# Fused attention, mixture of experts and gated MLP: a store that the first gathers no longer wait for, w_out loaded behind it, fillers moved

## The chip, the cores and the metric

The kernel runs on one core of a Trainium2 chip. The metric is the device time of one execution in microseconds (us). Before the change three runs took 814.79, 814.86 and 816.84 us; their median is 814.86 us.

## The reference

Three parts run one after the other: sparse attention (scores more than `tau` below the row's maximum are dropped), a mixture of eight experts in which a token may keep its predecessor's expert, and a gated MLP whose `w_sg` mixes the 576 tokens of a batch.

```python
scores = np.where(scores >= thresh, scores, -1e9)       # thresh: the row's maximum - tau
x = softmax(scores) @ v                                 # [4, 8, 576, 64] -> x [4, 576, 512]
...
e = fresh_e if s == 0 or local_gate[b, s] < 0.5 else prev_e
out[b, s] = p[e] * (np.maximum(x[b, s] @ w1[e], 0.0) @ w2[e])
...
h = gelu(x @ w_in); u, v = h[..., :512], h[..., 512:]
v_n = (v - mu) / np.sqrt(var + 1e-06) * g_ln
v_s = np.einsum('ts,bsd->btd', w_sg, v_n) + b_sg[None, :, None]
out = x + (u * v_s) @ w_out
```

## The kernel before

**Three stages.** Attention runs over pairs of heads and halves of the four batches (`Attn`); batches 0 and 1 are done first, 2 and 3 second. `Route` then sorts the 2304 tokens by expert into 22 tiles of 128 rows (`CAPS` gives the experts 5, 3, 3, 3, 2, 2, 2 and 2 tiles, in the order of a rank that is computed on the chip). `Tail.moe` gathers each tile's tokens from `x_dram` by an indirect DMA, multiplies by the expert's `w1` and `w2` as sums of three rounded products (a "high" and a "low" part of each operand), and stores each tile of results to the DRAM tensor `ys`. `Tail.mlp` gathers token tiles from `ys`, scales them by the gate's probability, transposes them and runs the gated MLP; it goes over two passes `p`: p = 0 is batches 0 and 1, p = 1 is batches 2 and 3, nine tiles of 128 tokens each.

**What sets the order.** All operations go into one graph (`Graph`, `Flow`) with an engine, a planned duration and a due time. `order` places them by a list schedule, and every engine then executes its own list strictly in that order. The waits between engines are put in afterwards by the framework, from what each instruction reads and writes, in the order in which the planner emits them. A gather from `ys` reads the whole tensor by this reckoning, since its rows are known only on the chip.

**The places that the change touches.**

- `Attn.keep`, two fillers on TensorE at the end of attention: six small products each of the identity with itself, whose result nobody reads.
- `Route.half` and `Route.rest`: small VectorE operations that count tokens by expert, rank the experts (`key`, `rank`), and turn the rank into tile numbers.
- `plain`, the first expert's first two tiles, unsplit: eight products "A1" (128x256) and eight "A2" (128x512), which fill TensorE while routing runs on VectorE. A1 reads the cell `c_78`, and a later chunk of `w2` is loaded into that cell.
- `second` and `put`: the second product of an expert and the store of its tile (`yst`). `self.yst` is the list of the 22 stores.
- `s_weights`: loads of the MLP's weights, among them two loads of `w_out` (from `wo32`, the copy in fp32) and their split into parts.
- `group`: for three token tiles each, the gather, the scaling `xpg` (VectorE), the transposes `xT` (TensorE), the split `xh` (ScalarE) and `xl` (VectorE), then per tile the product `vp` (twelve 128x512 matmuls) and a gelu (`sq`, `sqh`, `tanh`, `gelu`). The gather waits for all the stores:

```python
g.gather(W(need - self.P['mgth']), gth, r=[self.iu], w=[xu], deps=self.yst + [g.more], name="gth")
```

- `a.side`: during attention, zeros are stored to the spare tiles of `ys`, behind tile 22.

Most lines of the trace say L183, a helper through which `Tail`'s instructions go; there an instruction is told by its operands. `MF`, `MR`, `c` and `r` are parts of SBUF, `PS` is PSUM.

## Time and profile before

| | us | |
|---|---|---|
| median of three runs | 814.86 | 814.79 to 816.84 |
| the profiled execution | 814.26 | 0.60 under the median |
| its span, first to last instruction | 812.5 | 1.76 lies around it |
| TensorE (PE) busy | 771.8 | 95% of the span |
| VectorE (DVE) busy | 608.2 | 75% |
| ScalarE (ACT) busy | 461.5 | 57% |
| GpSimd (POOL) busy | 257.0 | 32% |
| mean granted clock of TensorE | 0.987 | 1 is 2.4 GHz, 0.5 is 1.2 GHz |

Times in the trace count from the first instruction. The page cuts the span into 40 slices and gives the busy share of each engine in tenths. TensorE stands at 9 nearly everywhere; the lowest slice, a 4, lies where the experts end and the MLP begins (some 569 to 589 us), and the granted clock is below 9 there alone.

### The profile page before, as it was taken

How to read it: one execution, taken by the hardware profiler on the slowest of the kernel's cores; microseconds unless marked ns; L12 is line 12 of the kernel's file. 1: busy time of each engine (PE TensorE's matmuls, PEld its weight loads, DVE VectorE, ACT ScalarE, POOL GpSimd, SP SyncE). 2: the span in 40 equal slices, each digit the busy share in tenths (PEclk: the TensorE clock that was granted, in tenths of full speed). 3: DMA queues.
4: the chain of work that ended last, by engine and by line, in shares of the span. 5: the costliest groups of instructions: out<-in, count | busy, mean ns of one | idle time of the engine just before them, and what ended most of it. 6: DMA issues, size and time to landing. Idle time of an engine off the chain costs nothing.

```text
span 812.5 us, 13654 instructions
## 1 busy us (share of the span) xinstructions
PE 771.8 (95%) x4813; PEld 658.3 (81%) x4814; DVE 608.2 (75%) x1293; ACT 461.5 (57%) x941; POOL 257.0 (32%) x348
## 2 busy tenths in 40 slices
PE   7899999999979999999999999999499999999997
PEld 4687877878667877598998988999388999899996
DVE  7999999999989985767668688774289753587732
ACT  5788988889848983354434455554336631256410
POOL 5232333332222300413524432224682143121410
PEclk9999999999999999999999999999799999999999
DMA  7232414453253012878576587644620012200011
GB/s 226 87 121 63 136 59 150 153 172 102 79 184 96 30 40 104 295 226 289 173 248 212 182 250 256 218 153 165 186 65 1 1 52 79 91 14 1 15 40 65
DMA packets 46909, 103.17 MB, mean 127 GB/s; under 512 B 7536, under 2 KB 7536, under 8 KB 46832
## 3 DMA queue, kind: packets, MB, share of 16 engines
q1 hardware_dynamic: 43632, 91.72, 34.3%
q0 software_dynamic: 3200, 10.49, 4.1%
q8 instruction: 40, 0.66, 0.3%
q14 instruction: 37, 0.30, 0.1%
HBM read 80.17 MB, written 22.02 MB: 126 GB/s over the span
## 4 chain that ended last, share of the span: by engine, by line
PE 52%; DVE 2%; issue 1%; DMA 1%; ACT 1%; POOL 0%; DVEq 0%
PE PS L183 52%; DVE MF L183 1%; DVE r L183 1%; DMA MF<-ys,MF 0%; ACT r L183 0%; ACT MF L183 0%; DVE c L183 0%; DMA ys<-MF 0%; DVE bs L183 0%; POOL MF L183 0%; DVE mv L183 0%; DVE rq L183 0%; DVE rqi L183 0%; DVEq L183 0%
## 5 line engine op out<-in xcount | busy, mean ns | idle before, releaser
L183 PE MATMUL PS<-r,r 128*128 128x512 f32 (+2 forms) x1512 | 298.3, 355 | 0.7 <-DVE MF L183 0.3
L183 PEld LDWEIGHTS PS<-r,r 128*128 128x128 f32 x1512 | 258.2, 190 | 32.4 <-DVE r L183 2.2
L425 PE MATMUL PS<-MR 128*128 128x288 f32 x640 | 114.3, 316 | 9.9 <-DVE MF L459 7.0
L459 DVE SCALAR_TENSOR_TENSOR MF<-PS,MF 128x576 f32<-128x576 f32 x144 | 116.8, 812 | 8.5 <-ACT MF L450 5.9
L450 ACT ACTIVATE MF<-PS,MF 128x576 f32<-128x576 f32 x144 | 107.5, 747 | 6.8 <-DVE MF L436 4.7
L430 DVE TENSOR_REDUCE MF<-PS 128x1 f32<-128x576 f32 x144 | 104.6, 752 | 8.8 <-PE PS L425 7.5
L425 PEld LDWEIGHTS PS<-MR 128*128 128x128 f32 x640 | 91.2, 191 | 18.8 <-DVE MF L459 11.3
L183 PE MATMUL PS<-MR,r 128*128 128x256 f32 (+2 forms) x616 | 101.6, 322 | 0.0
L183 PEld LDWEIGHTS PS<-MR,r 128*128 128x128 f32 x616 | 91.6, 188 | 8.1
L183 ACT ACTIVATE r<-PS 128x512 fp32r<-128x512 f32 (+2 forms) x102 | 49.1, 499 | 85.2 <-PE PS L183 82.1
L372 ACT ACTIVATE c<-PS 128x512 f32<-128x512 f32 (+1 forms) x160 | 82.5, 565 | 14.2 <-PE PS L479 13.9
L479 PE MATMUL PS<-ident,MF 128*128 128x128 f32 x576 | 81.7, 277 | 7.4 <-ACT c L372 7.0
L183 ACT ACTIVATE MF<-PS 128x512 f32<-128x512 f32 (+1 forms) x64 | 35.7, 558 | 77.1 <-PE PS L183 63.0
L479 PEld LDWEIGHTS PS<-ident,MF 128*128 128x128 f32 x576 | 65.8, 141 | 13.4 <-ACT c L372 11.0
L183 DVE TENSOR_TENSOR r<-c,r 128x1024 fp32r<-128x1024 f32 x42 | 56.2, 1368 | 16.4 <-ACT r L183 16.3
L183 DVE SCALAR_TENSOR_TENSOR r<-PS,r 128x384 fp32r<-128x384 f32 (+1 forms) x64 | 31.3, 489 | 45.3 <-ACT r L183 41.5
L183 DVE SCALAR_TENSOR_TENSOR MF<-MF,PS 128x384 f32<-128x384 f32 (+1 forms) x84 | 50.1, 606 | 16.2 <-ACT MF L183 15.7
L183 ACT ACTIVATE r<-c 128x1024 fp32r<-128x1024 f32 x46 | 46.8, 1055 | 15.1 <-PE PS L183 6.6
L183 POOL TENSOR_SCALAR MF<-MF 128x512 f32<-128x512 int32 x12 | 20.3, 1695 | 106.8 <-DVE MF L183 47.4
L404 POOL TENSOR_TENSOR MR<-c,MR 128x576 fp32r<-128x576 f32 x29 | 41.3, 1424 | 39.3 <-ACT MR L372 22.6
L183 ACT ACTIVATE r<-MF 128x256 fp32r<-128x256 f32 (+1 forms) x48 | 15.7, 359 | 62.2 <-DVE MF L183 62.2
L445 POOL TENSOR_TENSOR MF<-MF,cB 128x1 f32<-128x1 f32 x64 | 13.0, 204 | 117.4 <-DVE MF L430 108.1
(226 smaller groups left out, 1110.1 us busy)
## 6 DMA issues: line engine op xcount, KB each, us to landing
c<-in_w_dram SPq DMA_DIRECT2D x64, 512.0 KB, 4.8
c<-in_kP_dram SPq DMA_DIRECT2D x32, 288.0 KB, 3.1
c<-in_qP_dram SPq DMA_DIRECT2D x32, 288.0 KB, 3.1
ys<-MF SPq DMA_DIRECT2D x36, 256.0 KB, 3.5
x_dram<-c SPq DMA_DIRECT2D x6, 768.0 KB, 3.6
MF<-in_w_in_dram SPq DMA_DIRECT2D x8, 512.0 KB, 5.4
c<-in_vP_dram SPq DMA_DIRECT2D x12, 320.0 KB, 4.1
out_dram<-MF SPq DMA_DIRECT2D x12, 256.0 KB, 2.0
```

The source lines that it names most:

```text
L183: return lambda *a, **k: x(*[v(y) for y in a], **{n: v(y) for n, y in k.items()})
L372: self.nc.scalar.activation(out, src, AF.Copy, **k)
L404: e.tensor_tensor(l, self.raw(u)[1], h.bitcast(F32), op=ALU.subtract)
L425: self.nc.tensor.matmul(self.PS[:, banks[hf], 0:288], q, k[:, 288 * hf:288 * hf + 288], start=(n == 0), stop=(n == len(ops) - 1))
L430: self.nc.vector.tensor_reduce(m, self.tl[i]["s"], axis=AX.XY, op=ALU.max)
L445: self.nc.gpsimd.tensor_tensor(self.nbt(i)[:, 1:2], self.tl[i]["m"], self.cB[:, 1:2], op=ALU.add)
L450: self.nc.scalar.activation(e.rearrange("p (a b) -> p a b", a=2), t["s"], AF.Exp, bias=self.nbt(i)[:, 0:1], scale=0.125)
L459: self.nc.vector.scalar_tensor_tensor(w.rearrange("p (a b) -> p a b", a=2), t["s"], self.nbt(i)[:, 1:2], t["e"].rearrange("p (a b) -> p a ...
L479: self.nc.tensor.transpose(p[:, c, :], t["w"][:, z + c * 128:z + (c + 1) * 128], self.cst["ident"])
```

## The change

- The rank of the experts is broken at equal tile counts by the number of tokens of the first two batches instead of by the expert's number, so that the last expert in rank has few of them; if it has more than 128 of them its capacity falls by one tile (`f2`, `last`). So the last tile of the 22 holds tokens of batches 2 and 3 only. This is three small VectorE operations more.
- The gathers of pass p = 0 wait for all stores but the last one. Those of p = 1 wait for all, as before.
- The two loads of `w_out` also wait for the last store.
- `keep` is gone. In its place stand five fillers `idle` of the same six products, behind the last expert's last product.
- Zeros are stored to tile 21 as well (15 stores of zeros in place of 14; the first two go together).

```diff
-    KEEP = 6.949
...
-    def keep(self, banks):
-        x = self.cst["ident"].bitcast(BF16)
-        for _ in range(6):
-            self.nc.tensor.matmul(self.PS[:, banks[0], 0:256], x[:, 0:128], x[:, 0:256])
...
-        k = add("keep", "PE", 0.645, 18 * NPH / 2 * per + self.KEEP, lambda bk: self.keep(k.banks), [("av", NPH // 2 - 1, 1, 1)], 1)
-        k.users.append(add("keep2", "PE", 0.645, 18 * NPH / 2 * per + self.KEEP, lambda: self.keep(k.banks), [("rec", NPH // 2 - 1, 2)]))
...
-            k.append(op("DVE", 8, lambda: v.scalar_tensor_tensor(self.k0, fs, 1024.0, cst["cE"], op0=ALU.mult, op1=ALU.add), o))
+            k.append(op("DVE", 8, lambda: v.scalar_tensor_tensor(self.k0, fs, 1048576.0, ka, op0=ALU.mult, op1=ALU.add), o))
+            k.append(op("DVE", 8, lambda: v.tensor_scalar(self.f2, ca, 128.5, None, op0=ALU.is_gt), o))
...
-        o = op(8, lambda: v.scalar_tensor_tensor(key[:, :, 0], rt, 8.0, self.k0, op0=ALU.mult, op1=ALU.add), o)
+        o = op(8, lambda: v.scalar_tensor_tensor(key[:, :, 0], rt, 16384.0, self.k0, op0=ALU.mult, op1=ALU.add), o)
...
+        o3 = op(8, lambda: v.scalar_tensor_tensor(last, rank, 6.5, self.f2, op0=ALU.is_gt, op1=ALU.mult), o)
+        o1 = op(8, lambda: v.tensor_tensor(cap, cap, last, op=ALU.subtract), o1, o3)
...
+        p, o = Bank(), last
+
+        def idle():
+            x = ident.bitcast(BF16)
+            for _ in range(6):
+                nc.tensor.matmul(p.ap[:, 0:256], x[:, 0:128], x[:, 0:256])
+
+        for _ in range(5):
+            o = g.op("PE", 0.645, W(T + 6), idle, deps=[o], pw=p, name="idle")
+        p.first.users.append(o)
...
-            g.op("DQ", 1.46, V(P["wo"] - 6), ..., w=[wr], deps=self.conv, name="sld")
+            g.op("DQ", 1.46, V(P["wo"] - 6), ..., w=[wr], deps=self.conv + self.yst[-1:], name="sld")
...
-                g.gather(W(need - self.P['mgth']), gth, r=[self.iu], w=[xu], deps=self.yst + [g.more], name="gth")
+                g.gather(W(need - self.P['mgth']), gth, r=[self.iu], w=[xu], deps=(self.yst if p else self.yst[:-1]) + [g.more], name="gth")
...
+        zero = lambda *t: [nc.sync.dma_start(out=ys[k * 128:(k + 1) * 128, :], in_=z) for k in t]
+        a.side = [lambda: zero(NT - 1, NT)] + [lambda k=k: zero(k) for k in range(NT + 1, NT + NOV)]
```

**SP's list at the end of the experts.** SP issues the loads and stores. `ys<-MF` is a tile's store, `c_77<-wo` and `c_79<-wo` are the loads of `w_out`; `DMASW` semaphores count the indirect DMAs of GpSimd (0 and 1 are here the first two gathers of the MLP), `DMAHW` those of SP, eight in turn. Before:

```order
L183 DMA c_75<-in_w_sgT_dram 64x576
L183 DMA ys<-MF 128x512 [waits Activation_49]
L183 DMA c_77<-wo_60 128x2x512 [waits Pool_49]
L183 DMA ys<-MF 128x512 [waits Activation_49]
L183 DMA c_79<-wo_60 128x2x512 [waits DMAHW4_49,Pool_49]
```

and with the change:

```order
L183 DMA c_75<-in_w_sgT_dram 64x576
L183 DMA ys<-MF 128x512 [waits Activation_49]
L183 DMA ys<-MF 128x512 [waits DMASW1_49,DMASW0_49,Activation_49]
L183 DMA c_77<-wo_60 128x2x512 [waits Pool_49]
L183 DMA c_79<-wo_60 128x2x512 [waits DMAHW5_49,Pool_49]
```

Both loads of `w_out` moved behind the last store, and the last store waits for two gathers.

**GpSimd's list at the same place.** `MF<-ys` are gathers, `MR<-c` is the split of a part of `w_sg`. Before:

```order
L183 TENSOR_TENSOR MR<-c_79,MR 128x576 [waits DMAHW4_49,DMAHW7_49,PE_49,Activation_49]
L183 TENSOR_TENSOR MR<-c_78,MR 128x576 [waits DMAHW5_49,PE_49,Activation_49]
L183 DMA MF<-ys,MF 128x512 [waits DMAHW6_49,DMAHW3_49,DMAHW1_49]
L183 DMA MF<-ys,MF 128x512 x2
L183 DMA MF<-ys,MF 128x512 [waits DMASW3_49]
```

and with the change:

```order
L183 TENSOR_TENSOR MR<-c_79,MR 128x576 [waits DMAHW0_49,DMAHW5_49,PE_49,Activation_49]
L183 DMA MF<-ys,MF 128x512 [waits DMAHW7_49,DMAHW6_49,DMAHW2_49]
L183 DMA MF<-ys,MF 128x512
L183 DMA MF<-ys,MF 128x512 [waits DMAHW3_49]
L183 DMA MF<-ys,MF 128x512 [waits DMASW3_49]
```

The split of `c_78` moved behind the seventh gather. Counted in turn, the last store is the user of `DMAHW3` in both programs: before, the first gather names it; now the third does, and the first names `DMAHW2`, the store before the last.

**TensorE's and VectorE's lists at the end of attention.** On TensorE the routing's transposes and products (L1056, L1059, L1066, L1067 before) stand between the fillers (L305) and the products A1. Before:

```order
L1056 MATMUL PS<-ident,MF 9x9
L305 MATMUL PS<-ident 128x256
...
L1059 MATMUL PS<-ident,MF 128x9
L305 MATMUL PS<-ident 128x256
...
L1066 MATMUL PS<-MF 128x80
L1067 MATMUL PS<-MF 128x80
L183 MATMUL PS<-c_78,c_74 128x256
```

and with the change (each `c_78,c_74` begins one A1 of four matmuls):

```order
L1049 MATMUL PS<-ident,MF 9x9
L183 MATMUL PS<-c_78,c_74 128x256
...
L1052 MATMUL PS<-ident,MF 128x9
L183 MATMUL PS<-c_78,c_74 128x256
...
L1059 MATMUL PS<-MF 128x80
L1060 MATMUL PS<-MF 128x80
L183 MATMUL PS<-c_79,c_71 128x512 x4
L183 MATMUL PS<-c_78,c_71 128x512 x4
```

In VectorE's list one weight split moved into the routing, between the scan and the operation that follows it:

```order
L1050 TENSOR_REDUCE MF<-PS 9x1
L1051 SCALAR_TENSOR_TENSOR MF<-MF 9x128
L183 TENSOR_TENSOR r_3214<-c_79,r_3214 128x1024
L1053 TENSOR_SCALAR MF<-PS 128x9
L1054 TENSOR_TENSOR MF<-MF 128x8x9
```

Two A1 took the fillers' places, the A2 moved up ahead of the routing's turns, and the split that stood behind the routing stands in it.

## Rows read from the trace of the kernel before

**Rows 1.** Stages: us, busy us of PE, PEld, DVE, ACT, POOL, clock, DMA share, GB/s.

```profile
347.78:575.13 227.35, 227.09 (x1292) 205.62 (x1292) 156.87 (x222) 107.08 (x161) 81.00 (x59) 1.00 0.65 216
575.13:585.99 10.86, 0.00 (x0) 0.03 (x1) 0.48 (x1) 5.79 (x8) 5.28 (x6) 0.70 0.66 203
593.23:610.74 17.51, 16.93 (x94) 15.00 (x92) 15.76 (x29) 8.65 (x17) 15.58 (x20) 1.00 0.08 27
```

**Rows 2.** The chain of waits that ended last: start us, us, what.

```profile
610.74 18.25 PE PS L183 x94
```

**Rows 3.** Timeline of SP's queue at the last stores.

```profile
574.42 0.58 SPq L183 DMA_DIRECT2D ys<-MF  x1
575.04 0.43 SPq L183 DMA_DIRECT2D c<-wo  x1
575.77 0.32 SPq L183 DMA_DIRECT2D ys<-MF  x1
```

**Rows 4.** DMA, us to landing: stores at 550.3, 574.4, 575.7; gather at 583.3.

```profile
ys<-MF SPq DMA_DIRECT2D x1, 256.0 KB, 2.0
...
ys<-MF SPq DMA_DIRECT2D x1, 256.0 KB, 2.8
...
ys<-MF SPq DMA_DIRECT2D x1, 256.0 KB, 5.5
...
MF<-ys,MF POOLq DMA_INDIRECT x1, 3.5
```

**Rows 5.** Timeline of POOL: gathers 1, 3 and 6, then the splits.

```profile
581.99 1.03 POOL L183 DMA_INDIRECT MF<-ys,MF  x1 [4.19 <-issue]
...
584.58 0.95 POOL L183 DMA_INDIRECT MF<-ys,MF  x1 [0.30 <-issue]
...
588.50 0.95 POOL L183 DMA_INDIRECT MF<-ys,MF  x1 [0.31 <-issue]
...
593.23 7.41 POOL L183 TENSOR_TENSOR MR<-c,MR 128x576 fp32r<-128x576 f32 x5
600.72 4.94 POOL L183 TENSOR_TENSOR r<-c,r 128x1024 fp32r<-128x1024 f32 x2
```

**Rows 6.** Timeline of DVE: sixth scaling, first gelu step, eighth scaling.

```profile
592.32 0.48 DVE L183 TENSOR_SCALAR MF<-MF 128x512 f32<-128x512 f32 x1 [0.71 <-DMA MF<-ys,MF]
594.29 0.69 DVE L183 SCALAR_TENSOR_TENSOR MF<-MF,PS 128x512 f32<-128x512 f32 x1 [1.49 <-ACT MF L183]
...
601.27 2.13 DVE L183 TENSOR_SCALAR c<-c,MF 128x512 f32<-128x512 f32 x1
```

**Rows 7.** Timeline of PE: first vp, then second and third vp with the first up.

```profile
588.49 5.13 PE L183 MATMUL PS<-r,r 128*128 128x512 f32 x12
...
593.82 9.92 PE L183 MATMUL PS<-r,r 128*128 128x512 f32 x48
```

**Rows 8.** As rows 1, where the granted clock rises again.

```profile
593.00:593.20 0.20, 0.20 (x2) 0.18 (x1) 0.00 (x0) 0.00 (x0) 0.20 (x1) 0.84 0.90 123
```

**Rows 9.** Timelines of PE, DVE and ACT at the end of attention.

```profile
316.38 1.89 PE L183 MATMUL PS<-c,c 128*128 128x256 f32 x8
...
318.30 0.83 PE L305 MATMUL PS<-ident 128*128 128x256 bf16 x6
...
327.70 1.29 PE L1204 MATMUL PS<-MF 128*128 128x20 bf16 x36 [0.31 <-DVE MF L1197]
...
342.14 4.74 PE L183 MATMUL PS<-r,MR 128*128 128x384 f32 x24
...
319.39 0.17 DVE L1060 TENSOR_SCALAR MF<-PS 128x9 int32<-128x9 int32 x1 [0.32 <-PE PS L1059]
...
332.79 1.22 DVE L183 TENSOR_TENSOR r<-c,r 128x1024 fp32r<-128x1024 f32 x1
...
339.03 1.89 DVE L183 TENSOR_TENSOR r<-PS,r 128x512 fp32r<-128x512 f32 x3
...
318.59 1.05 ACT L183 ACTIVATE r<-c 128x1024 fp32r<-128x1024 f32 x1
```

More of the change, by code (lines that the diff above doesn't have):

```diff
@@ L998, in __init__ @@
         self.pg = self.sp[:, 1, :]
-        self.es, self.first, self.least, self.k0, self.c2, self.d2, self.rc = m([128, 1]), m([128, 8]), m([128, 8]), m([128, 8]), m([128, 8]), m([128, 8]), m([128, 8], I32)
+        self.es, self.first, self.least, self.f2, self.k0, self.c2, self.d2, self.rc = m([128, 1]), m([128, 8]), m([128, 8]), m([128, 8]), m([128, 8]), m([128, 8]), m([128, 8]), m([128, 8], I32)
         self.pe = h2(lambda: m([128, 9, 8]))
@@ L1161, in rest @@
         ovx, cE, rc = cst["ovx"], cst["cE"], self.rc
-        rt, key, cmp_, rank, cap, base, ov, oc, dl, pk = t([128, 8], I32), t([128, 8, 1]), t([128, 8, 8]), t([128, 8]), t([128, 8]), t([128, 8]), t([128, 8]), t([128, 9]), t([128, 8]), t([128, 1, 8, 1])
+        rt, key, cmp_, rank, last, cap, base, ov, oc, dl, pk = t([128, 8], I32), t([128, 8, 1]), t([128, 8, 8]), t([128, 8]), t([128, 8]), t([128, 8]), t([128, 8]), t([128, 8]), t([128, 9]), t([128, 8]), t([128, 1, 8, 1])
         osel, pt, bT, cT, dT, os_, tl = t([128, 2, 8, 9]), t([128, 18], I32), t([128, 18], I32), t([128, 18], I32), t([128, 18], I32), t([128, 18]), t([128, 18, 1], BF16)
@@ L1397, in mm @@
                             nc.tensor.matmul(p.ap, x[:, f, :], y[:, s], start=(f == 0 and n == 0), stop=(f == 7 and n == 2))
-                g.op("PE", pe(512, 6), W(T), mm, r=[hu[2 * ch], hu[2 * ch + 1]] + wc, pw=p, name="L2")
+                R["last"] = g.op("PE", pe(512, 6), W(T), mm, r=[hu[2 * ch], hu[2 * ch + 1]] + wc, pw=p, name="L2")
                 T += pe(512, 6)
@@ L1486, in moe @@
                 T = second(t, hh[:, :, c], hl[:, :, c], W8, hu, T)
+                last = R["last"]
             for _ in range(2):
@@ L1585, in s_weights @@
             src = w_out[k * 256:(k + 1) * 256, :].rearrange("(a p) d -> p a d", p=128)
-            g.op("DQ", 1.46, V(P["wo"] - 6), lambda raw=raw, src=src: nc.sync.dma_start(out=raw.rearrange("p (a d) -> p a d", a=2), in_=src), w=[wr], deps=self.conv, name="sld")
+            g.op("DQ", 1.46, V(P["wo"] - 6), lambda raw=raw, src=src: nc.sync.dma_start(out=raw.rearrange("p (a d) -> p a d", a=2), in_=src), w=[wr], deps=self.conv + self.yst[-1:], name="sld")
             c = slice(2 * k, 2 * k + 2)
@@ L1953, in fused_attention_moe_gmlp_kernel @@
         a = Attn(tc, ctx, qP, kP, vP, wgl, tau, x_dram, cst)
-        a.side = [lambda k=k: nc.sync.dma_start(out=ys[k * 128:(k + 1) * 128, :], in_=z) for k in range(NT, NT + NOV)]
+        zero = lambda *t: [nc.sync.dma_start(out=ys[k * 128:(k + 1) * 128, :], in_=z) for k in t]
+        a.side = [lambda: zero(NT - 1, NT)] + [lambda k=k: zero(k) for k in range(NT + 1, NT + NOV)]
         a.extra = route_consts(tc, cst)
```

## The prediction

> **What bounds the kernel now.** I read the stages first, then the chain of waits, then the timelines of the five engines around the places that the chain names. While the experts run, TensorE works 227.09 of 227.35 us at full clock, and behind 610.74 us the chain is TensorE's own again [rows 1, 2]: what is won or lost ahead of either stretch passes through to the end. The span loses its time between them. From 575.13 us TensorE does nothing for 10.86 us, and the mean clock of that gap, 0.70, says that it stood at 2.4 GHz for (0.70 - 0.50) / 0.50 x 10.86 = 4.3 us and then at 1.2 GHz [rows 1]. The gap is a relay: the last tile's store is issued at 575.77 and lands 5.5 us later, since a load of w_out went ahead of it at 575.04 [rows 3, 4]; 581.27 us. The first gather starts 0.72 us behind that, at 581.99 [rows 5]. Then the first product vp takes 5.13 us at the low clock, where twelve of the 48 matmuls behind it take 2.5 [rows 7]; the clock rises at 593.1 [rows 8]. From 593.23 to 610.74 us two engines are nearly full, TensorE with 16.93 and VectorE with 15.76 of 17.51 us [rows 1]. So there VectorE has to start earlier too, or TensorE's lead is of no use.
>
> **The change, step by step: the store and the gathers.** The store before the last is issued at 574.42 and lands in 2.8 us [rows 3, 4], at 577.22. With the same 0.72 us the first gather starts at 577.94, 4.05 us earlier. That is what the edit says. The lists say more. The framework counts a gather as a reader of all of `ys`; so the last store, emitted behind two gathers, now waits until both have landed, and the third gather, emitted behind the store, waits for it. Gather 2 starts 1.03 + 0.30 us behind the first [rows 5], at 579.27, and lands 3.5 us later [rows 4], at 582.77. Only then the last store goes out. Its price isn't in the trace at this place; its bounds are 2.0 and 5.5 us, the extremes of the stores [rows 4]. I take 2.8, the row nearest to it: there, as here, a load of w_out follows the store, while the 5.5 had one ahead. It lands at 585.57, and gather 3 starts at 586.29, **1.71 us later than before** (584.58 [rows 5]); gathers 4 to 9 follow it.
>
> [...]
>
> **Who waits for gather 3 and 6.** TensorE has its first two tiles early, but the third tile's transposes stand ahead of the second vp in its list, so it stops behind the first vp, by 587 us at the latest at full clock, until 586.29 + 3.8 + 0.5 = 590.6 (landing and scaling as of gather 6: 588.50 to 592.32, 0.48 [rows 5, 6]). VectorE's list is unchanged, and there the sixth scaling stands ahead of the first gelu step. Gather 6 starts at 588.50 + 1.71 = 590.21, its scaling ends at 590.21 + 3.82 + 0.48 = 594.51, and the gelu step follows, which began at 594.29 [rows 6]: 0.2 us **later**. By the bounds of the last store it is 0.6 us earlier (2.0) to 2.9 later (5.5); if the store before it lands in 2.0 as well, 1.4 earlier.
>
> **VectorE against GpSimd.** The eighth scaling took 2.13 us at 601.27 where the sixth took 0.48, while GpSimd split a part of w_out from 600.72 [rows 5, 6]: 1.65 us lost. GpSimd reaches that split later now: 1.71 us, and one w_sg split of 7.41 / 5 = 1.48 us moves from ahead of the gathers to between them. Its four remaining splits run from 596.4 to 602.3. The eighth scaling, at 601.5, meets the last of them and waits 0.8 us. I take a gain of 0.8, between none and 1.65. Both together: 0.2 - 0.8 = **-0.6 us** at 610 us, between -3.0 and +2.9.
>
> **The fillers** cost nothing: TensorE has nothing else to do behind its last product. Five groups of 0.83 us at most [rows 9] end by 579.3, 2.6 us or more ahead of the first transposes, so they hide under the gathers. The loads of w_out go out behind the last store, collide with gather 3 at most by a part of a us, and their split isn't wanted before the MLP's end. ScalarE's halves of it stand between the gelu's steps now, where VectorE is the later one; nothing.
>
> **The end of attention.** Removing `keep` takes some 1.5 us of fillers (two groups of 0.83, overlapping) from a full TensorE. But each group's place is taken by an A1 of 1.89 us, and the routing's products queue behind it [rows 9]. VectorE's L1060 ran at 319.39. Now a weight split of 1.22 us stands ahead of it, which waits for ScalarE until 318.59 + 1.05 = 319.64: L1060 runs at 320.9, 1.5 us later. The second A1 adds 0.2, the two new operations on this chain (0.17 us each, like L1060) 0.3: **the routing ends 2.0 us later**. Its product at 327.70 goes to 329.7; TensorE bridges that with A2 from behind it. The gathered tiles' last split ended at 339.03 + 1.89 = 340.92, 1.22 us before the experts' product at 342.14 needed it [rows 9]; it now ends at 340.92 + 2.0 - 1.22 (the split that moved away) = 341.7. TensorE alone would be ready at 342.14 - 1.5 = 340.6. The later one decides: 341.7, a gain of **0.4 us**, between 1.5 (the routing is not late) and a loss of 0.8 (it is late and the moved split gives nothing back).
>
> **The rest.** One more store of zeros among 14 and one small operation during attention: a third of a us either way at most, taken as nothing; SP has idle time between loads.
>
> **The sum.** 814.26 (the profiled execution) - 0.6 - 0.4 = 813.26. The median stands 0.60 above that execution, so the forecast is **813.9 us**, 0.1% less. A measurement of this kernel tells 0.3%, or 2.4 us, from no change: below 812.4 is faster, above 817.3 slower.
>
> **Rivals.** (1) *The gathers are all free.* If the wait in the lists were met early, all nine gathers would start 4.05 us earlier, the sixth scaling would end at 588.75, and VectorE would begin 5.5 us earlier: 809.0 us. For it speaks the edit, against it the two lists. Chance 0.06.
>
> (2) *The clock stays low.* TensorE now pauses twice, some 3 us in front of the first transposes and some 4 behind the first vp, and in the trace the clock fell 4.3 us after work ended. If it falls in the second pause, vp 2 runs from 591.7 for 5.13 us to 596.8, where it ended at 593.82 + 2.5 = 596.3. That alone costs little; but if vp 3 is slow as well it ends 3 us late, and the time is 817. In the trace the clock came back 4.6 us after the first vp began [rows 7, 8], which would be in time for vp 3. Chance 0.14. The Trainium skill ("TensorE: Matmul & The Clock Gate", section "HAM oscillation") warns of just this, pauses between bursts that throttle the array again each time; the trace agrees in so far as its one long pause did.
>
> (3) *The last store is slow* and the kernel gets slower. It goes out while gather data and w_out share the queues. If it takes 5.5 us as before, gather 3 starts at 589.0, the gelu 2.9 us late, TensorE pauses over 6 us, and the end is at 814.86 - 0.4 + 2.9 = 817.4, up to 818 with the low clock. It decides from a landing of about 3.5 us, where the MLP's gain is gone. For it: the row of 5.5; against: nothing is ahead of the store in SP's list now. Chance 0.12.
>
> **How the numbers follow.** My forecast's case has 0.60, spread over 811.5 to 815.8 by the bounds of its stores, the scaling and the routing; some 0.18 of it lies below 812.4. The remaining 0.08 is for what I don't see, to both sides. Faster: 0.18 + 0.06 + 0.03 = 0.27. Slower: 0.06 of (3), 0.03 of (2), 0.02 of the rest = 0.11. Same: 0.62. A range of 811.0 to 817.0 leaves out the free gathers, the upper half of (2) and (3) and a little of the main case.
>
> **What would show it.** In the new profile: gather 1 near 578 and gather 3 near 586, with SP's last store between them, issued when gather 2 has landed; TensorE with two pauses in place of one of 10.9 us; the first gelu step within a us of 594; the eighth scaling under 2 us; no fillers at 318, L1060's successor near 321, the experts' first product near 341.7. I am wrong if gather 3 starts by 582, if the first gelu step stands before 592, or if the clock is low behind 597.

## The result and the profile after: 0.6% slower

The changed kernel took 820.89 us (median of 22 runs, 815.68 to 823.91), the kernel before 815.61 in the same comparison (22 runs, 814.24 to 818.4): a ratio of 1.0057 with a 95% interval of 1.0045 to 1.007. That is slower, where 813.9 us had been forecast and a range up to 817.0. The profiled execution of the new kernel took 822.08 us, its span 820.1, at a mean granted clock of 0.983 (before: 812.5 and 0.987).

To see where 7.6 us of span went, both spans are cut at the same four events: the start of the last store of `x` (X), the experts' first gathered product (L1, 24 matmuls 128x384), the end of their last product (E), and the point M from which the chain is TensorE's own. First the stretches of the kernel before, with the columns of [rows 1]; its stretches 342.14 to 347.78 and 347.78 to 575.13 (the second is in [rows 1]) meet at a conditional branch, `with tc.If(number > 0)`:

```profile
314.80:342.14 27.34, 26.62 (x170) 16.28 (x168) 21.56 (x87) 10.50 (x20) 8.44 (x7) 1.00 0.68 233
342.14:347.78 5.64, 4.74 (x27) 4.21 (x25) 0.56 (x1) 1.09 (x2) 0.00 (x0) 1.00 0.50 187
575.13:610.74 35.61, 23.82 (x112) 20.16 (x112) 20.08 (x37) 15.63 (x27) 26.55 (x31) 0.81 0.39 116
610.74:812.50 201.76, 197.45 (x1128) 179.67 (x1128) 123.29 (x254) 76.57 (x156) 46.30 (x111) 1.00 0.11 36
```

The same stretches of the kernel after:

```profile
0.00:316.36 316.36, 293.41 (x2090) 234.76 (x2092) 285.57 (x695) 250.59 (x576) 94.59 (x142) 0.98 0.35 112
316.36:345.90 29.54, 27.08 (x157) 15.91 (x156) 22.04 (x89) 10.51 (x20) 7.94 (x7) 0.94 0.66 207
345.90:353.96 8.06, 4.43 (x25) 4.14 (x25) 0.95 (x2) 1.58 (x3) 0.00 (x0) 0.97 0.52 167
353.96:582.64 228.68, 228.53 (x1294) 207.20 (x1295) 156.17 (x222) 106.55 (x160) 81.39 (x59) 0.99 0.65 214
582.64:618.48 35.84, 26.99 (x144) 22.12 (x141) 21.27 (x37) 15.45 (x27) 23.96 (x31) 0.90 0.37 115
618.48:820.10 201.62, 197.43 (x1128) 179.74 (x1128) 123.47 (x254) 76.35 (x156) 48.59 (x111) 1.00 0.11 36
```

Attention is 316.36 - 314.80 = 1.56 us longer. In it the clock stood low for 10.2 us at 227 us where it stood low for 3.4 before; that differs from run to run of kernels that are alike there (6.8 and 3.4 us in the two traces of e4 below), so it isn't put down to the change. X to L1 is 2.20 longer, L1 to E 236.74 in place of 232.99, that is 3.75 longer, E to M 0.23 longer, the rest 0.14 shorter. **The MLP's start, for which the change was made, gave nothing, and the largest part of the loss lies behind the experts' first product**, where the prediction had put no term.

That place, on TensorE's timeline. Before, then after (start us, us, what, idle before it and what ended it):

```profile
337.38 5.32 PE L183 MATMUL PS<-c,c 128*128 128x512 f32 x12
342.14 4.74 PE L183 MATMUL PS<-r,MR 128*128 128x384 f32 x24
347.78 0.94 PE L183 MATMUL PS<-r,MR 128*128 128x384 f32 x4 [0.90 <-PEq L1655]
```

```profile
339.48 1.76 PE L183 MATMUL PS<-ident,MF 128*128 128x128 f32 x8 [1.94 <-DMA MF<-x_dram,inv]
341.03 2.97 PE L183 MATMUL PS<-c,c 128*128 128x512 f32 x4
...
344.27 1.88 PE L183 MATMUL PS<-c,c 128*128 128x512 f32 x4
345.90 4.43 PE L183 MATMUL PS<-r,MR 128*128 128x384 f32 x24
353.96 2.26 PE L183 MATMUL PS<-r,MR 128*128 128x384 f32 x6 [3.63 <-PEq L1663]
```

`PEq L1655` (now L1663) is TensorE's sequencer at that branch; it leads to the spare tiles, and its body is skipped here. Behind it TensorE idles 0.90 us before and 3.63 after. What it waits for can be read from the DMA packets of a queue named "instruction", 16 KB on queue q8: the fetch of code. Its rows in the stretch 345 to 346 us of before, and 349.9 to 352.4 of after (packets, MB, share of 16 engines):

```profile
q8 instruction: 1, 0.02, 6.0%
```

```profile
q8 instruction: 1, 0.02, 5.9%
```

6.0% of 16 engines over 1 us is one packet of 0.96 us; 5.9% over 2.5 us is one of 2.35. (After, another 16 KB packet of this queue went just ahead of it, from 349.61 to 350.70.) By the packet records the packet in question starts at 345.24 before and at 349.98 after, and TensorE goes on 2.54 and 3.98 us after that start, in both 1.6 us after the landing. In all 17 traces of this document that last step is 1.46 to 1.73 us, however long the pause. Before, the packet starts 1.64 us ahead of the end of the product (346.88), so most of the fetch is hidden under that product. After, it starts 0.35 us ahead of the end (350.33) and takes longer.

Whether TensorE comes to the branch later is seen in its sequencer's row for the branch, listed under PEld, before and then after (duration in ns, start in us):

```profile
L1655 PEldq COMPARE_BRANCH  x1: 3412/3412/3412, 344.2 to 344.2; - x1
```

```profile
L1663 PEldq COMPARE_BRANCH  x1: 6138/6138/6138, 347.7 to 347.7; - x1
```

By the records it begins at 344.20 and 347.66, in both 2.67 us ahead of the product's end. So measured from the product the sequencer is as early as before. The fetch is not: its packet starts 1.04 us behind the branch's start before, and 2.32 after. In the 1.5 us from that start the transfers were these (columns of [rows 1], before and after), and the share of queue q0, which moves the gathers, was 3.5% and 36.4%:

```profile
344.20:345.70 1.50, 1.50 (x11) 1.50 (x10) 0.35 (x1) 0.49 (x1) 0.00 (x0) 1.00 0.60 231
```

```profile
347.66:349.16 1.50, 1.50 (x11) 1.50 (x10) 0.00 (x0) 0.49 (x1) 0.00 (x0) 1.00 0.81 298
```

With the change the gathers of `x` are late and still under way when the fetch is due. TensorE's clock falls behind that pause:

```profile
339.80:343.20 3.40, 3.40 (x11) 2.07 (x9) 3.22 (x4) 1.19 (x2) 2.27 (x2) 0.50 0.79 247
353.40:356.80 3.40, 2.84 (x9) 2.87 (x10) 0.56 (x1) 0.13 (x1) 0.94 (x1) 0.51 0.46 92
589.00:595.80 6.80, 5.03 (x15) 3.82 (x16) 1.66 (x3) 1.19 (x2) 1.84 (x2) 0.50 0.69 214
```

The 72 matmuls behind the branch take 14.07 us at it; at full clock they take 12.72 to 12.76 (table below). The first of these rows is a low clock behind the wait of 1.94 us for a gather; it makes one A2 2.97 us long instead of 1.88. The third is the MLP's start.

**The MLP's start** came as the lists said. GpSimd's gathers 1 and 3, VectorE, the GpSimd split beside VectorE's last row, and the landing of the last two stores (the first issued at 581.95, the second at 591.31):

```profile
586.31 1.03 POOL L183 DMA_INDIRECT MF<-ys,MF  x1 [2.86 <-DMA ys<-MF]
593.65 0.94 POOL L183 DMA_INDIRECT MF<-ys,MF  x1 [5.07 <-DMA ys<-MF]
```

```profile
601.72 0.68 DVE L183 SCALAR_TENSOR_TENSOR MF<-MF,PS 128x512 f32<-128x512 f32 x1
...
608.62 1.17 DVE L183 TENSOR_SCALAR c<-c,MF 128x512 f32<-128x512 f32 x1
...
612.02 1.52 DVE L183 TENSOR_SCALAR rq<-mv 128x3 f32<-128x3 f32 x1
```

```profile
611.12 2.39 POOL L183 TENSOR_TENSOR r<-c,r 128x1024 fp32r<-128x1024 f32 x1
```

```profile
ys<-MF SPq DMA_DIRECT2D x1, 256.0 KB, 4.1
...
ys<-MF SPq DMA_DIRECT2D x1, 256.0 KB, 2.1
```

From E, gather 1 starts at 3.67 us and gather 3 at 11.01 (before 9.45 [rows 5]); the first gelu step at 19.08 (before 19.16 [rows 6]). The eighth scaling is 0.96 us shorter [rows 6], but `rq`, three columns wide and 0.16 us before (at 605.64), takes 1.52 beside a split on GpSimd and ends with it (613.54 and 613.51 us).

### The profile page after: what moved, and what is told of

The parts are those of the page before. It is cut to its first block, busy times and chain, and to the rows that moved or that the text cites. A ratio compares the mean times of both kernels' runs of the same rounds, so it can differ in the third digit from the quotient of the medians.

```text
span 820.1 us, 13698 instructions
## 1 busy us (share of the span) xinstructions
PE 777.9 (95%) x4831; PEld 663.9 (81%) x4832; DVE 609.5 (74%) x1296; ACT 461.0 (56%) x941; POOL 256.5 (31%) x348
## 4 chain that ended last, share of the span: by engine, by line
PE 51%; DVE 2%; issue 1%; DMA 1%; POOL 1%; ACT 0%; SPq 0%; POOLq 0%; DVEq 0%
PE PS L183 51%; DVE MF L183 1%; DMA ys<-MF 1%; POOL MF L183 0%; DMA MF<-ys,MF 0%; DVE r L183 0%; POOL r L183 0%; DVE bs L183 0%; ACT MF L183 0%; DVE rq L183 0%; ACT r L183 0%; SPq L183 0%; DVE c L183 0%; DVE mv L183 0%; DVE rqi L183 0%
## 5 line engine op out<-in xcount | busy, mean ns | idle before, releaser
L183 PE MATMUL PS<-r,MR 128*128 128x384 f32 (+1 forms) x288 | 47.5, 325 | 3.8 <-PEq L1663 3.6
```

Of the source, the lines that this page charges most:

```text
L183: return lambda *a, **k: x(*[v(y) for y in a], **{n: v(y) for n, y in k.items()})
```

## The experiments

The traces stand in one table, in us, one trace for each row; e4_same is e4_swap again, after_same is after again, e11_same is e11_split again. Gather: start of the experts' first gather less X. L1: its start less X. Cover: L1's start less the end of VectorE's last split of gathered tiles (row `r<-PS,r 128x512`); near 0 L1 waits for its data. Fetch: from the start of the branch on TensorE's sequencer to the start of the fetch's packet. DMA: busy share of the 16 DMA engines in the 1.5 us from that start (a packet counts whole where it starts). Pause: TensorE's idle time at the branch. x72: the matmuls behind it. L1-E and E-M as above. Ratio: to the kernel before, of the same comparison.

| kernel | gather | L1 | cover | fetch | DMA | pause | x72 | L1-E | E-M | ratio |
|---|---|---|---|---|---|---|---|---|---|---|
| before | 14.75 | 27.34 | 1.22 | 1.04 | 0.60 | 0.90 | 12.76 | 232.99 | 35.61 | 1 |
| after | 17.37 | 29.54 | 0.06 | 2.32 | 0.81 | 3.63 | 14.07 | 236.74 | 35.84 | 1.0057 |
| e1_keep | 15.02 | 27.97 | 1.58 | 1.25 | 0.55 | 1.06 | 12.74 | 232.86 | 34.60 | 0.9998 |
| e2_nokeep | 17.21 | 28.34 | 0.06 | 2.26 | 1.01 | 2.14 | 12.74 | 234.00 | 36.22 | 1.0039 |
| e5_keep_all | 15.02 | 27.66 | 1.27 | 1.04 | 0.63 | 1.35 | 12.72 | 234.64 | 35.96 | 1.0007 |
| e4_swap | 17.39 | 27.88 | 0.06 | 2.81 | 1.01 | 2.64 | 14.30 | 236.18 | 36.20 | 1.0038 |
| e4_same | 17.37 | 27.82 | 0.05 | 3.12 | 0.98 | 3.16 | 14.30 | 236.35 | 35.89 | 1.0052 |
| e14_cover | 17.37 | 29.17 | 1.89 | 1.71 | 0.90 | 1.66 | 12.74 | 233.58 | 36.03 | 1.0058 |
| e6_defer | 17.37 | 27.70 | 0.06 | 4.49 | 0.84 | 4.50 | 14.30 | 237.75 | 35.29 | 1.0040 |
| e9_keep_defer | 15.02 | 27.91 | 1.52 | 1.06 | 0.58 | 1.16 | 12.74 | 233.04 | 34.41 | 0.9994 |
| after_same | 17.43 | 29.38 | 0.05 | 1.84 | 0.88 | 1.92 | 14.32 | 235.22 | 35.74 | 1.0023 |
| e11_same | 17.38 | 29.61 | 0.05 | 1.74 | 1.00 | 1.87 | 14.29 | 235.11 | 35.68 | 1.0014 |
| e13_before_split | 16.14 | 34.04 | 3.23 | 1.08 | 0.51 | 0.95 | 12.73 | 234.94 | 35.73 | 1.0021 |
| e11_split | 17.36 | 29.51 | 0.05 | 1.84 | 0.96 | 0.82 | 12.74 | 234.15 | 36.19 | 1.0009 |
| e10_keep_defer_shi | 15.01 | 31.59 | 1.72 | 1.46 | 0.50 | 1.26 | 12.72 | 233.12 | 34.88 | 0.9994 |
| e12_keep_noidle | 15.01 | 31.60 | 1.67 | 1.02 | 0.50 | 1.02 | 12.72 | 234.49 | 35.25 | one run |
| e7_later | 17.38 | 29.45 | 0.05 | 1.03 | 0.16 | 1.28 | - | 240.41 | 36.14 | 1.0099 |

The branch begins 2.67 us ahead of the product's end in thirteen of the 17 traces, 2.62 in e14, 2.40 in e11_same, 2.33 in e7, and 3.71 in e11_split, whose L1 ran partly at the low clock. The fetch starts 1.02 to 1.46 us behind the branch's start in the kernels with `keep` and in e7, where the DMA engines are 0.16 to 0.63 busy, and 1.71 to 4.49 us behind it in the others, where they are 0.81 to 1.01 busy.

L1-E of e5, e12 and e13 has besides one wait of TensorE for VectorE, far behind the branch, of 1.0, 1.0 and 1.4 us, which neither before nor e4 or e14 have.

In two of the six comparisons the kernel before took 819.4 and 819.63 us, against 815.6 to 816.4 in the others. There VectorE's second `CAST inv` (L1208 of before) starts late, though the product that it reads has ended. In e13 and in after_same:

```profile
338.07 0.17 DVE L1214 CAST inv<-PS 128x14 int32<-128x14 f32 x1 [4.34 <-remote]
```

```profile
337.46 0.17 DVE L1204 CAST inv<-PS 128x14 int32<-128x14 f32 x1 [2.66 <-PE PS L183]
```

The wait was 0.71 to 0.78 in the other comparisons; in these two it was 4.19 to 4.34 in kernels with the fillers `keep`, 1.87 to 2.66 in kernels without. The kernel before wasn't traced in these comparisons; if it has that wait too, the ratios there (after_same, e11, e13, e10, e12) come out nearer to 1, so they are compared among themselves only. What VectorE waited for is not shown, and the cause stays open.

### Which part of the change costs the time

**e1_keep**: the change, with the fillers `keep` put back.

```diff
+        k = add("keep", "PE", 0.645, 18 * NPH / 2 * per + self.KEEP, lambda bk: self.keep(k.banks), [("av", NPH // 2 - 1, 1, 1)], 1)
+        k.users.append(add("keep2", "PE", 0.645, ...
```

> The changed kernel with the two fillers `keep` and `keep2` put back at the end of attention; all else of the change stays. Theory A (the loss lies at the end of attention and at the conditional branch behind it, and comes from the fillers' removal alone): 815.6 to 816.6 us, at most 0.1% above the kernel before; TensorE goes on 0.9 us behind the branch, the experts' first product is within 0.8 us of 342.1. Theory B (the loss comes from the gathers, the last store and VectorE's contention at the start of the MLP): 819 to 821 us, as in the changed kernel.

**e2_nokeep**: the kernel before, with `keep` alone taken away.

```diff
-        k = add("keep", ...
-        k.users.append(add("keep2", ...
```

> The kernel before with only the two fillers `keep` and `keep2` taken away. Theory A: 4 to 6 us above the kernel before (ratio 1.005 to 1.007), with the load of 512 KB behind the first tile's store in SP's list and some 3.5 us of pause behind the branch. Theory B: within 1 us of the kernel before, or up to 0.4 us faster.

Measured: e1 816.0 us, 0.9998 (0.9984 to 1.0011); e2 818.84, 1.0039 (1.0025 to 1.0054), less than the 4 to 6 us expected. Both stand against 816.35 of the same comparison. Taking two fillers (0.83 us each [rows 9]) from TensorE costs (1.0039 - 1) x 816.35 = 3.2 us by itself, and putting them back takes the whole loss away. That the fillers' removal is what costs is shown both ways. In e2's trace the pause is 2.14 us and the clock doesn't fall behind it, so e2 has less of the loss than after (1.0039 and 1.0057, with intervals that overlap). TensorE behind the branch, e1 and then e2:

```profile
350.88 12.74 PE L183 MATMUL PS<-r,MR 128*128 128x384 f32 x72 [1.06 <-PEq L1671]
```

```profile
351.72 12.74 PE L183 MATMUL PS<-r,MR 128*128 128x384 f32 x72 [2.14 <-PEq L1653]
```

**e5_keep_all**: before, with the change's routing operations, zeros and five fillers behind the experts; gathers and `w_out` as before.

```diff
-            k.append(op("DVE", 8, lambda: v.scalar_tensor_tensor(self.k0, fs, 1024.0, cst["cE"], ...
+            k.append(op("DVE", 8, lambda: v.scalar_tensor_tensor(self.k0, fs, 1048576.0, ka, ...
+            k.append(op("DVE", 8, lambda: v.tensor_scalar(self.f2, ca, 128.5, None, op0=ALU.is_gt), o))
...
+            o = g.op("PE", 0.645, W(T + 6), idle, deps=[o], pw=p, name="idle")
```

> The kernel before with only the three routing operations, the store of zeros and the five fillers behind the experts: the first gathers wait for all stores and w_out is loaded early, as before. Theory A: the stretch from the experts' last product to the end of the relay at the MLP's start is 35.6 us as before, 1 us more than with the gathers freed; the routing costs 0.3 to 0.6 us; 816 to 816.7 us against 815.9 of the kernel before. Rival (the gain with the gathers freed is that of the fillers alone): that stretch is 34.6 us here too.

Measured: 816.55 us against 816.01, 1.0007 (0.9993 to 1.0021). The routing operations cost 15.02 - 14.75 = 0.27 us at the first gather, and nothing that can be told at the end.

### Why the missing fillers cost more than they took

**e4_swap**: after, with one row of SP's list moved. Without `keep` the planner also put the store of the first expert's first tile ahead of the last of the experts' first weight loads, which then went out at 345.32 us (before: the last of seven, by 339.6); here the store stands behind the load again.

```diff
+            a, b = self.swap
+            seq.remove(a)
+            seq.insert(seq.index(b) + 1, a)
...
+                    if (k, i) == (1, 3):
+                        g.swap = self.yst[0], wr[0].w[-1]
```

> The changed kernel with one row moved: on SP, the store of the experts' first tile goes behind the load of 512 KB that it had been moved ahead of; every other engine's list is the same. Theory A: the load lands before the branch again, the pause of 3.6 us behind the branch falls to about 1 us and the low clock after it goes away: 3 to 4 us below the changed kernel, 817 us. Rival (the pause belongs to the branch whatever is in flight, and only varies): no difference, 820 to 821 us.

Measured: 819.31 us, 1.0038 (1.0024 to 1.0052); again as e4_same, below, 820.92, 1.0052 (1.0032 to 1.0072). That one load isn't in the way any more, the pause is still 2.64 and 3.16 us and the clock still falls; the rival holds. It speaks only of this load: the DMA engines are 1.01 and 0.98 busy behind the branch in these two traces, half of it gathers. Against 1.0057 of after, 0.05 to 0.2% hung on that row, which the intervals don't tell from nothing.

**e7_later**: after, with the branch moved from behind the second to behind the sixth product of the first expert (the collecting of these operations into `early` is left out here).

```diff
+            n = seq.index(self.more.deps[0])
+            x = [o for o in seq[n:] if o in self.early]
+            seq = seq[:n] + x + [o for o in seq[n:] if o not in self.early]
```

> The changed kernel with the conditional branch of the experts moved from behind the second gathered product L1 to behind the sixth, on TensorE, VectorE and ScalarE; the loads and gathers keep their order. Theory C (new: the fetch of the code behind the branch starts when an engine's sequencer has issued all that stands ahead of it; a product that waited for late data takes the sequencer's lead away, so the fetch is no longer hidden behind running products): behind six products the lead is there again, the pause behind the branch is 0.9 to 1.2 us instead of 2.1 to 4.5, no low clock follows it, the time is 2 to 3.5 us below the changed kernel, 817.5 to 819 us. Rival (the pause is that of a fetch at any place of the program): it stays at 2.5 us, 820 to 821 us. Loads behind the branch start 8 us later; should the second expert need them, its products wait and the time is above 821.

Measured: 824.7 us, 1.0099 (1.0071 to 1.0127).

```profile
359.75 4.40 PE L183 MATMUL PS<-r,MR 128*128 128x384 f32 x24 [1.28 <-PEq L1671]
369.10 2.93 PE L183 MATMUL PS<-r,r 128*128 128x512 f32 x6 [4.95 <-DVE r L183]
```

```profile
363.94 4.63 DVE L183 TENSOR_TENSOR r<-c,r 128x1024 fp32r<-128x1024 f32 x4 [4.37 <-ACT r L183]
```

The pause at the branch falls to 1.28 us and the clock stays up there, as expected, but not for the reason that was expected. The sequencer has no more lead than before:

```profile
L1671 PEldq COMPARE_BRANCH  x1: 3452/3452/3452, 356.1 to 356.1; - x1
```

It begins 2.33 us ahead of the product's end (358.46). What is better is the fetch, which starts 1.03 us later (357.16), at a place where the DMA engines are 0.16 busy. So without fillers too the fetch is quick at a quiet place. In all the kernel is slower: the weight splits of VectorE and ScalarE stand behind the branch too; they run only after it, and the second layer waits 4.95 us for them.

**e11_split**, **after_same**, **e11_same**: after, with VectorE's weight split moved back behind the routing (the row that the prediction gave 1.2 to 1.5 us); the kernel after itself; and the first again beside it.

```diff
+        D = [o for o in seq if o.eng == "DVE"]
+        x, = (D[j] for j in range(1, len(D) - 1) if [o.name for o in D[j - 1:j + 2]] == ["rt", "wlo", "rt"])
+        n = next(o for o in D[D.index(x) + 1:] if o.name == "wlo")
+        seq.remove(x)
+        seq.insert(seq.index(n), x)
```

> The changed kernel with one row moved on VectorE: the weight split that stands in the routing goes behind the routing, where it stood before; every other engine's list is the same. Theory D (of the two things that the fillers' removal does to the routing, the split in VectorE's list is the larger): the routing ends some 1.2 us earlier, the experts' first product starts 27.3 to 27.6 us behind the last store of attention, TensorE's pause behind the branch falls to 1 to 1.5 us, and the time is 2 to 4 us below the changed kernel, 817 to 819 us. Rival (the products A1 in the fillers' places hold the routing): nothing comes back, since VectorE then waits for TensorE's transposes; 820 to 821 us.

> The changed kernel itself, beside the next two kernels and the kernel before on one chip: ratio 1.004 to 1.007 to the kernel before, TensorE's pause behind the branch 2 to 4.5 us.

> The changed kernel with the weight split on VectorE moved back behind the routing, on the same chip as the changed kernel. Theory D (the split in the routing is what costs): 2 to 4 us below the changed kernel, ratio to the kernel before 1.001 to 1.003. Rival (the earlier ratio of 1.0009 came from a kernel before that was slow on that chip, and the split is worth nothing because VectorE then waits for TensorE's products A1): within 1 us of the changed kernel, ratio 1.004 to 1.007.

**e13_before_split**: the opposite, the kernel before (with `keep`) and that one split moved into the routing.

```diff
+        x = next(o for j, o in enumerate(D) if o.name == "wlo" and D[j - 1].name == "rt")
+        h = max(seq.index(d) for d in x.deps)
+        n = next(o for o in D if o.name == "rt" and seq.index(o) > h)
+        seq.remove(x)
+        seq.insert(seq.index(n), x)
```

> The kernel before, fillers and all, with one row moved on VectorE: the weight split goes into the routing, to the very place where the change has it; every other engine's list is the same. Theory D: L1060 runs some 1.2 us later, the experts' first product 1 to 1.5 us, and TensorE's pause behind the branch grows to 1.5 to 2.5 us: 2 to 3 us above the kernel before, ratio 1.002 to 1.004. Rival (the fillers' places on TensorE decide): within 0.5 us of the kernel before.

Measured: e11_split 820.6 against 819.63, 1.0009 (0.9996 to 1.0022), and its pause 0.82, since its L1 ran partly at low clock (6.01 us for 24 matmuls) and hid more of the fetch. In the next comparison e11_same was 820.33, 1.0014 (1.0003 to 1.0025), after_same 821.11, 1.0023 (1.0005 to 1.0041), e13 821.54, 1.0021 (1.0009 to 1.0033), all against 819.4; after_same is below the 1.004 to 1.007 expected, beside a kernel before that was slower than elsewhere. Taken out of the kernel after, the split gives nothing back at the first gather, 17.38 against 17.43, as the rival had it. Put into the kernel before, it makes the first gather 16.14 - 14.75 = 1.39 us later. Its ratio is as expected, but the pause of 1.5 to 2.5 us did not come: it is 0.95. Its L1 at 34.04 is to be read beside the 31.59 and 31.60 of e10 and e12, which also have `keep` and the wait before `CAST inv`: 2.4 us later, and that ahead of L1. What holds the routing there is seen on TensorE and VectorE of after:

```profile
319.86 2.00 PE L183 MATMUL PS<-c,c 128*128 128x256 f32 x8
321.78 0.22 PE L1052 MATMUL PS<-ident,MF 9*128 9x9 f32 x1
```

```profile
320.16 0.47 DVE L1051 TENSOR_TENSOR_SCAN MF<-MF 9x128 f32<-9x128 f32 x1
321.22 1.22 DVE L183 TENSOR_TENSOR r<-c,r 128x1024 fp32r<-128x1024 f32 x1 [0.59 <-ACT r L183]
322.36 0.16 DVE L1053 TENSOR_SCALAR MF<-PS 128x9 int32<-128x9 int32 x1
...
324.04 0.23 DVE L1064 TENSOR_TENSOR MF<-PS,MF 128x72 f32<-128x72 f32 x1 [0.45 <-PE PS L1060]
```

The scan ends at 320.63, and its product on TensorE could run then; it stands behind a pair of A1 (2.00 us, where the filler took 0.83 [rows 9]) and runs at 321.78. The split ends 0.4 us after that product. So the A1 alone hold the first gather by the whole 2.6 us (e11; 0.27 of it are the routing's new operations, by e5), the split alone by 1.39 (e13), and both together by no more than the A1. A kernel that takes out the A1 alone was not run.

**e14_cover** and **e4_same**: e4, with one A2 (and the copy of its tile on ScalarE) moved behind the third token tile's transposes, so that two A2 and not one stand between the last gathered tile and L1; no filler; and e4 again beside it.

```diff
+        x, y, (t, u) = E("A2")[-2], E("ysb")[-2], (E("xT")[-1], E("xh")[-1])
+        for o in (y, x):
+            seq.remove(o)
+        seq[seq.index(u) + 1:seq.index(u) + 1] = [x, y]
```

> The kernel after with the store moved behind the load (as in e4) and, besides, the first experts' seventh A2 (and the copy of its tile on ScalarE) moved behind the third token tile's transposes, so that two A2 in place of one (about 1.9 us more of work) stand between the last gathered tile and the experts' first gathered product. No filler is added. Theory (the fetch of the code behind the branch is hidden only as far as TensorE's sequencer leads; the work that stood as cover in front of L1 gave the lead): the first gathered product begins 0 to 1.9 us later than in e4 (27.9 us behind the store of x there), the pause behind the branch falls from 2.6 to 0.9 to 1.4 us, the product behind it runs in 12.7 us in place of 14.3, so that the stretch from the experts' first product to their last falls from 236.2 to 233 us. In all 0.998 to 1.000 of e4_same, by what the later start takes back. Rival (the pause is the branch's own price without fillers, or the transfers'): pause 2.1 us or more, the stretch 235 us or more, and in all equal to or up to 0.2% above e4_same.

> e4 again on the same chip, as the measure for e14_cover. If this chip is like the first: 1.0038 of the kernel before, pause 2.1 to 2.7 us. If VectorE's wait of some 3.5 us shows here as on two other chips, the ratio is 1.001 to 1.002 and the pause 1.8 to 2.0.

Measured: e14 820.36 us, 1.0058 (1.004 to 1.0076), e4_same 820.92, 1.0052 (1.0032 to 1.0072), both against 816.39. e14's TensorE, and then that of e4_same:

```profile
341.85 4.12 PE L183 MATMUL PS<-c,c 128*128 128x512 f32 x8
345.40 4.74 PE L183 MATMUL PS<-r,MR 128*128 128x384 f32 x24
351.81 12.74 PE L183 MATMUL PS<-r,MR 128*128 128x384 f32 x72 [1.66 <-PEq L1678]
```

```profile
342.78 4.47 PE L183 MATMUL PS<-r,MR 128*128 128x384 f32 x24
350.42 14.30 PE L183 MATMUL PS<-r,MR 128*128 128x384 f32 x72 [3.16 <-PEq L1670]
```

With cover and without a filler the pause falls from 3.16 to 1.66 us (0.9 to 1.4 had been expected), the clock stays up behind it, and L1-E falls by 236.35 - 233.58 = 2.77 us. The lead doesn't grow by it: the branch begins 2.62 us ahead of the product's end, 2.67 in e4_same. The fetch starts 1.71 us behind the branch in place of 3.12, now that the gathers have almost all landed. A fall of that size is also within what the same kernel shows twice (3.63 in after, 1.92 in after_same), so one trace doesn't prove it. L1 itself comes 29.17 - 27.82 = 1.35 us later, X itself is 1.27 us later in e14's trace (more of the low clock in attention), and neither the two spans (816.6 us both) nor the medians differ. What the branch gives back, the later start takes.

### What the MLP's start could give

**e6_defer**: after, with the last store waiting for six gathers, so that gathers 3 to 6 don't wait for it.

```diff
-                g.gather(W(need - self.P['mgth']), gth, ... deps=(self.yst if p else self.yst[:-1]) + [g.more], name="gth")
+                d = g.gather(W(need - self.P['mgth']), gth, ... deps=(self.yst if p else self.yst[:-1]) + [g.more], name="gth")
+                if not p and t < 5:
+                    self.yst[-1].deps += d.deps
```

> The changed kernel with the last store of the experts put behind the first six gathers of the MLP instead of behind two, so that these six wait for nothing but the store before it. Theory A: gather 3 starts 2.5 us behind gather 1, the sixth scaling and the first gelu step some 3.5 us earlier, the time 2.5 to 4 us below the changed kernel, 817 us. Rival (VectorE and TensorE are full behind it anyway, or the first vp at the low clock decides): below 1 us of gain, 820 us.

Measured: 819.07 us, 1.004 (1.0024 to 1.0056). The stores and gathers do as wanted: gather 3 starts 6.2 us behind E in place of 11.0, and the first gelu step 15.4 in place of 19.1. VectorE, and then ScalarE, show why E-M falls by 0.55 us only:

```profile
595.56 0.69 DVE L183 SCALAR_TENSOR_TENSOR MF<-MF,PS 128x512 f32<-128x512 f32 x1 [0.85 <-ACT MF L183]
...
600.71 0.69 DVE L183 SCALAR_TENSOR_TENSOR MF<-MF,PS 128x512 f32<-128x512 f32 x1 [2.12 <-ACT MF L183]
```

```profile
599.13 1.06 ACT L183 ACTIVATE r<-c 128x1024 fp32r<-128x1024 f32 x1 [2.21 <-DMA c<-wo]
```

The loads of `w_out` go out behind the later store, ScalarE's half of their split stands ahead of a gelu step in its list, and VectorE's third gelu waits for it.

**e9_keep_defer** and **e10_keep_defer_shi**: `keep` and the deferred store; e9 with the loads of `w_out` ahead of the store again, e10 with ScalarE's halves moved to where their other halves stand.

```diff
+            seq = seq[:n] + w + [o for o in seq[n:] if o not in w]      # e9: w, the loads of w_out; n, the store
...
+        for h, l in getattr(self, "late", ()):                          # e10
+            seq.remove(h)
+            seq.insert(seq.index(l), h)
```

> The changed kernel with the fillers put back at the end of attention, the last store behind six gathers, and the two loads of w_out ahead of that store instead of behind it. Theory A: the attention's end as before the change, and behind the experts' last product the first gelu step after some 15.5 us instead of 19.1; ScalarE no longer waits for w_out there; 2 to 3 us below the run with the fillers put back, 813 to 814 us, ratio 0.996 to 0.998. Rival (VectorE's contention with GpSimd takes it back): as with the fillers alone, 816 us.

> The changed kernel with the fillers put back at the end of attention, the last store behind six gathers, the loads of w_out behind that store, and ScalarE's halves of its split moved to just ahead of GpSimd's. Theory A: nothing on ScalarE waits for w_out between the gelu steps, the gathers have the queues for themselves; from the experts' last product to the end of the relay 33 us instead of 34.6 with the fillers alone: 814 to 814.8 us, ratio 0.997 to 0.999. Rival (behind the gathers VectorE and GpSimd take it back): 816 us, as with the fillers alone.

**e12_keep_noidle**: e1 without the five fillers behind the experts, one profiled run.

```diff
-        for _ in range(5):
-            o = g.op("PE", 0.645, W(T + 6), idle, deps=[o], pw=p, name="idle")
```

> The changed kernel with the fillers put back at the end of attention and the five fillers behind the experts taken away. Theory: they shorten the time at the low clock by at most one product vp (0.6 us between 5.1 and 4.5 us); without them the stretch from the experts' last product to the end of the relay is 34.6 to 35.6 us. Rival (they do nothing): 34.6 us.

Measured: e9 814.9 against 816.01, 0.9994 (0.998 to 1.0008); e10 818.82 against 819.63, 0.9994 (0.998 to 1.0007), E-M 34.9; e12 820.29 in its one run, E-M 35.3. With `keep` in place the MLP's start is 0.3 to 1.2 us shorter than before's 35.61 (e1, e9, e10, e12), which a measurement of the whole doesn't show; e9 and e10 miss the 0.996 to 0.998 and 0.997 to 0.999 that were expected. None of the kernels beats the kernel before by more than its interval.

## Why the prediction was wrong, point by point

- **The step that failed is "the end of attention"**, with its result "341.7, a gain of 0.4 us, between 1.5 and a loss of 0.8". Measured from X, L1 came 2.20 us later, and it was followed by a loss of 3.75 us up to E, for which the step had no term. The routing was forecast 2.0 us late and was 17.37 - 14.75 = 2.62; L1060's successor ran at 322.36 - 1.56 = 320.8, as said. Of the 2.20 us, 1.84 are not in e6 (L1 at 27.70), whose rows on TensorE and SP stand there in the same order: in after TensorE waited 1.94 us for a gather and its clock fell, in e6 it waited 1.63 and the clock stayed up. In the traces without that low clock and without the wait before `CAST inv` L1 is 0.4 to 1.0 us late (e6, e4, e4_same, e2).
- **The term that was missing** stands behind L1: TensorE's pause at the branch, 0.90 us before, was taken as it was. It grew by 2.73 us, and the low clock behind it made the 72 matmuls 1.31 longer; L1 itself was 0.31 shorter. Together that is 3.73 of the 3.75 us, out of the 7.60 - 1.56 = 6.04 that aren't attention's. The pause is longer because the code fetch starts later behind the branch, and in after its packet takes longer too (2.35 in place of 0.96 us). It is not that TensorE's sequencer lost a lead, as the expectations of e7 and e14 have it: the lead is 2.67 us with `keep` and without. Nor does the cover of 1.22 us [rows 9] decide: without cover the pause is anything from 0.82 to 4.50 us.
- **What delays the fetch** is argued and not shown. The transfers in flight fit all 17 traces, with e7 as the nearest test: no fillers, a quiet place, 1.03 us. The two longest pauses (after and e6) have besides another 16 KB packet of the same queue just ahead of the fetch. But in all kernels without `keep` save e7 VectorE also reaches its branch ahead of TensorE (345.79 and 347.66 in after; 345.99 and 344.20 before), so that a fetch for VectorE may go first, and no run separates the two.
- **The fillers.** "Removing `keep` takes 1.5 us from a full TensorE" was true of TensorE's busy time and wrong of its list: their place went to pairs of A1, 2.00 us in place of 0.83, and A2 was used up ahead of the gathers. The lists in the section on the change show both; the lengths stood in [rows 9]. That either of A1 and the split holds the routing, and A1 the longer, was shown by e11 and e13.
- **SP's list** was read at the experts' end only. The store that moved ahead of a load at 345 us wasn't seen; by e4 it costs 0.05 to 0.2%, which is not clear of noise.
- **The store and the gathers** were right in their mechanism. The forecast counts in before's time, where E is 575.13; it was 582.64, 7.51 us later. Less that, gather 1 is at 578.80 (577.94 forecast), gather 3 at 586.14 (586.29), the first gelu step at 594.21 (594.5 forecast). The two stores took 4.1 and 2.1 us where 2.8 was forecast for each (bounds 2.0 and 5.5); that the two errors cancel is luck. The 4.1 us stood behind other transfers, the 2.1 had none ahead of it.
- **VectorE against GpSimd** gave 0.96 us at the eighth scaling (0.8 forecast), and took 1.36 at `rq`, a row to which the prediction gave no term. So the forecast of -0.6 us at the MLP's start became +0.23. Five splits stood behind the gathers and not the four of the prediction; the scaling meets one of them either way.
- **The fillers behind the experts and the loads of `w_out`** cost nothing here, as said. e6 shows the condition: with the gelu 3.7 us earlier and the load behind a later store, the load is 2.2 us late for ScalarE.
- **The rivals.** The free gathers did not come. The last store was quick, 2.1 us. The clock was low at 589.0 to 595.8, over the first vp alone, and up again before the second at 599.30; the fall in the second pause, which the second rival needed, did not come. At the end of attention it fell twice, behind pauses of 1.94 and 3.63 us, and there it cost: the warning of the Trainium skill ("TensorE: Matmul & The Clock Gate", section "HAM oscillation") of pauses between bursts fits this place, to which the prediction didn't apply it. The time came from none of the rivals.

## What to carry to other kernels

Before idle filler work is taken away, look at what moves into its place and what that makes late. Here A1 moved in, the experts' gathers came 2.6 us later, and they were still under way where TensorE's code was to be fetched. A conditional branch in the middle of a stage is a place of its own in the sum: what is seen of its fetch depends on the product that runs meanwhile and on how soon the fetch starts. Here it started soonest where little else was moving; but leave nothing on the far side that others wait for soon (e7). Compare the new lists at every place where they differ, not only where the edit points.

## What was unexpected of the hardware

- **A branch around skipped code costs a fetch.** TensorE went on 1.46 to 1.73 us after its 16 KB packet had landed, in all 17 traces. The packet took 0.96 us when it was quickest and 2.35 at most, in after; from its start to TensorE's next product 2.47 to 3.98 us passed. What is seen of it is that, plus the 1.02 to 4.49 us from the branch's start to the packet's, less the part under the product that still runs (2.67 us in most traces). The same kernel differs from run to run: 3.63 and 1.92 us of pause in after and after_same.
- **The clock fell behind short pauses, but not by their length alone:** behind 1.87, 1.92, 2.64, 3.16, 3.63 and 4.50 us at the branch, and not behind 2.14 (e2) or any of 1.66 and less.
- **A wait of VectorE before `CAST inv`**, of 4.19 to 4.34 us in kernels with `keep` and 1.87 to 2.66 without, is there in all traces of two comparisons, and 0.71 to 0.78 in all the others. In these two comparisons the kernel before, which wasn't traced there, took 0.4% longer. The cause was not found.
